# One core of Trainium2, a Fourier layer and an MoE layer: more weight pieces fetched and split in the prologue, one filler more there, and GpSimd's sums for batch 2 held back

## The chip, the cores and the metric

The kernel runs on one core of a Trainium2 chip. The metric is the device time of one execution in microseconds (us), taken as the median of several runs. A core has five engines that work through queues of their own, each in order: TensorE (PE, with its weight loads as PEld), VectorE (DVE), ScalarE (ACT), GpSimd (POOL) and SyncE (SP, which here only issues DMAs). DMAs are also issued from ScalarE's and GpSimd's queues.

## What is computed

For 8 batches of 3008 x 256 numbers, the reference takes a real Fourier transform along the sequence, multiplies by complex weights, adds a bias, shrinks every value towards zero by 0.01, and transforms back. The result, 24064 tokens, goes through a layer of the kind h = x w_in, out = (h cos h) w_out.

```python
X = np.fft.rfft(x, axis=1)
Yr = Xr @ w_r - Xi @ w_i + b_r
Yi = Xr @ w_i + Xi @ w_r + b_i
Yr = np.sign(Yr) * np.maximum(np.abs(Yr) - lam, 0.0)
y = np.fft.irfft(Y, n=x.shape[1], axis=1)
h = x @ w_in
g = h * np.cos(h)
return (g @ w_out).astype(np.float32)
```

The MoE weights w_in (256 x 2048) and w_out (2048 x 256) come as 64-bit floats.

## The kernel before, in words

**Numbers.** Products of 32-bit accuracy are made of three products of a coarser type: each operand is split into a high part (a rounding copy, mostly on ScalarE) and a low part (the operand minus its high part, on VectorE by `rest`, line 328, or on GpSimd by `rest_pool`, line 325).

**The MoE weights** are prepared on the chip, in 16 pieces: 8 of w_in, then 8 of w_out. A piece is loaded raw by GpSimd's queue (`load_f64`, line 255; 512 KB), then `split_f64` turns its 64-bit words into a high and a low 32-bit part, with an Abs on ScalarE (line 268), six instructions on VectorE (lines 269 to 276), a copy on ScalarE (line 277) and a subtraction on VectorE (line 328). Its scratch tile `wa` lies in the buffer "z" for the even ones of the early pieces and in "y" otherwise. Ten pieces (`W_EARLY`) are loaded in the prologue, into the buffers "xp" (`XP_BUFS`, six) which the first batch's input occupied before; piece k + 3 is asked for when piece k is split. Nine are split between the steps of the first batch's transform (`W_AT`) and one more after it. The other six are loaded into the tiles "at", "z" and "Xh" (`load_late_pieces`), and their loads wait for "pc", the transposing products of the first MoE tile; they are split ahead of the steps f = 0, 1, 3, 5, 8 and 11 of that tile (`W_LATE`).

**The order of instructions** comes from three sources. The program emits them in the order of its generators: while one batch's MoE runs, `ahead` lets the next batch's transform come in pieces, with costs that are written by hand. A scheduler then orders each engine's queue by its own estimate of when operands are ready, so an instruction can come well ahead of where it was emitted. Against this, `tc.issue_after(x)` keeps what is emitted under it behind x on x's engine (order only, no wait for x to end). `floor()` (line 317) applies it to the instructions of the MoE step two back: the copy gh on ScalarE, the subtraction gl, and a product; while fewer than two steps exist it holds nothing. Splits are issued under `floor()` and behind `mark["act"]` and `mark["dve"]`, ScalarE's and VectorE's last instructions of the first batch's transform.

**One MoE step** (`moe_step`, `second`) takes 128 of the 2048 hidden columns f for a tile of 512 tokens: six products into ph (lines 923 to 925), on ScalarE u (932), VectorE u (933), ScalarE's sine (935), VectorE's product with h (936), ScalarE's gh (938), gl on VectorE or, for even f, on GpSimd; three steps later six products into po (lines 905, 906, 909). There are 6 tiles of 16 steps per batch.

**The transform.** `stage_a(b)` transforms a batch's input in six blocks c. For batch 1 the blocks are bursts of 16 products each (line 377, tiles pa): three are made in the prologue, as fillers for TensorE (`alone`), three in the first tile (`ahead`, k = 3, 4, 5). Their stores, but for the first, are held until "pc" (`held`, `release`). From batch 2 on GpSimd first makes the sum and the difference of the two halves of a block (`fold`, lines 450 and 451), from tiles xt that its own queue loads (line 442); blocks c + 2 are loaded after the burst of block c. `stage_b(b)` holds the rest: `forward`, `combine` (splitting into Xh and Xl, with sums on GpSimd, lines 594 to 612), `wmix` (lines 660 to 662 and the shrinking, 684 and 686), its own `fold` with GpSimd's lines 699 to 711 and VectorE's transposes (716, 717), and `inverse`/`spread` (739, 740). `stage_c` loads a tile bt, transposes it by products pc (line 377) and splits it into xTh (ScalarE, line 890) and xTl (VectorE, line 891).

Of the kernel before, what the change touches and what calls it, by code (L numbers as in the profile page):

```python
# [13 lines left out]
F32 = mybir.dt.float32  # L14
# [3 lines left out]
U32 = mybir.dt.uint32  # L18
# [10 lines left out]
NFC = FF // 128  # L29
NTT = 6  # L30
SKEW = 3
XP_BUFS = 6
W_AT = (8, 16, 24, 32, 40, 48, 56, 64, 74)
W_ORDER = tuple(range(16))
W_EARLY = 10
W_LATE = (0, 1, 3, 5, 8, 11)
W_AHEAD = 3
POOL_GL = (0, 2)
WARM = 7
# [137 lines left out]
def tile_body(ctx: ExitStack, tc, x, w_r, w_i, b_r, b_i, w_in, w_out,  # L177
              c_fq, c_sig, c_f3, c_ff, c_if, c_iw, c_sgn, out):
    nc = tc.nc
# [80 lines left out]
    def split_f64(k, hi, lo, raw):  # L260

        pair = raw.rearrange("p (n t) -> p n t", t=2)
        v = pair[:, :, 1]
        maq = wk.tile([128, 3, 512], F32, tag="z" if k < W_EARLY and k % 2 == 0 else "y", name="wa", bufs=1)
        m, a, q = (maq[:, j] for j in range(3))
        mu, au, qu = m.bitcast(U32), a.bitcast(U32), q.bitcast(U32)
        ve = nc.vector
        nc.scalar.activation(m, v.bitcast(F32), AF.Abs)
        ve.tensor_scalar(out=m, in0=m, scalar1=F64_TINY, scalar2=F64_HUGE, op0=ALU.max, op1=ALU.min)
        ve.tensor_scalar(out=qu, in0=mu, scalar1=0x07FFFFFF, scalar2=3,  # L270
                         op0=ALU.bitwise_and, op1=ALU.logical_shift_left)
        ve.scalar_tensor_tensor(out=au, in0=v, scalar=0xC0000000, in1=qu,
                                op0=ALU.bitwise_and, op1=ALU.bitwise_or)
        ve.tensor_scalar(out=qu, in0=au, scalar1=0xFF800000, scalar2=None, op0=ALU.bitwise_and)
        ve.scalar_tensor_tensor(out=q, in0=pair[:, :, 0], scalar=2.0 ** -52, in1=q, op0=ALU.mult, op1=ALU.mult)
        ve.tensor_tensor(out=a, in0=a, in1=q, op=ALU.add)
        nc.scalar.copy(hi, a)
        rest(lo, a, hi)
# [15 lines left out]
    raws, mark = [], {}  # L294
# [4 lines left out]
            raws.append(load_f64(raw, words(W_ORDER[len(raws)])))  # L299

    def load_late_pieces():
        for tag, n in (("at", 2048), ("z", 2048), ("Xh", 2304)):
            t = wk.tile([128, n], U32, tag=tag, name="raw", bufs=1)
            for k in range(2):
                raws.append(load_f64(t[:, 1024 * k:1024 * k + 1024], words(W_ORDER[len(raws)]), "pc"))

    def moe_w():
        for k, w in enumerate(W_ORDER):
            load_pieces(k + W_AHEAD)
            with floor(), tc.issue_after(mark["act"].ins), tc.issue_after(mark["dve"].ins):  # L310
                split_f64(k, *halves(w), raws[k])
            yield

# [3 lines left out]
    def floor():  # L317

        ctx = ExitStack()
        for ins in steps[-2] if len(steps) > 1 else ():  # L320
            ctx.enter_context(tc.issue_after(ins.ins))
        return ctx
# [111 lines left out]
    def stage_a(b):  # L434
# [10 lines left out]
                    behind(ins, mark["pc"].ins, "first tile")  # L445

        def fold(c):
            ev[c] = wk.tile([128, 2, 256], F32, tag="xe", name="xe", bufs=2)
            lo, hi = ld[c][:, :, 0], ld[c][:, :, 1]
            nc.gpsimd.tensor_tensor(out=ev[c], in0=lo, in1=hi, op=ALU.add)  # L450
            nc.gpsimd.tensor_tensor(out=lo, in0=lo, in1=hi, op=ALU.subtract)
# [51 lines left out]
        def alone():  # L503
            load(0)
            load(1)
            yield 0.0
            for tag in ("Xh", "Xl"):
                t = wk.tile([128, 2304], F32, tag=tag, name="x1", bufs=1)
                for k in range(2):
                    c = len(ld)  # L510
                    ld[c] = t[:, 1024 * k:1024 * k + 1024].rearrange("p (i g d) -> p i g d", i=2, g=2)
                    nc.sync.dma_start(t[:, 1024 * k:1024 * k + 1024], x[b, :, 1024 * c:1024 * (c + 1)])
            for c in range(3):
                yield from burst_of([c])

        def begin():
# [437 lines left out]
    with ExitStack() as first:  # L954
        pool["pro"] = first.enter_context(tc.tile_pool(name="pro", bufs=1))
        pool["a0"] = early.enter_context(tc.tile_pool(name="a0", bufs=1, side="right"))
        idle = pool["pro"].tile([128, 512], F32R, tag="st", name="idle", bufs=1)
        nc.vector.memset(idle.bitcast(F32), 0.0)
        turn0 = pool["pro"].tile([128, 1], F32, name="turn0", bufs=1)
        nc.scalar.activation(turn0, idle[:, :1].bitcast(F32), AF.Sin)  # L960

        def warm(n):
            p = ps.tile([128, 512], F32, tag="o0", name="pz", bufs=1)
            for _ in range(n):
                mm(p, idle[:, :128], idle, start=True, stop=True)

        warm(WARM)
        fi[0] = pool["pro"].tile([96, 2, 96], F32, name="fi", bufs=1)
        stage_a0()
        load_constants()  # L970
        stages["a"] = stage_a(1)
        side_a = stages["a"].alone()
        next(side_a)
        split = 0
        stages[0] = stage_b(0)
        for i, _ in enumerate(stages[0].first()):
            if i == 0:
                load_pieces(2)
                with tc.issue_after(mark["x0"].ins):
                    load_split_constants()  # L980
            if i == 4:
                with tc.issue_after(mark["a0", 1].ins):
                    sum_fourier_w()
                    bounds()
            if split < len(W_AT) and i >= W_AT[split]:
                next(mw)
                split += 1
        for _ in side_a:
            pass
        next(mw)  # L990
        with tc.issue_after(mark["act"].ins), tc.issue_after(mark["dve"].ins):
            split_fourier_w()
        for _ in range(len(W_AT) + 1, W_EARLY):
            next(mw)
    del pool["pro"]
    pool["mo"] = ctx.enter_context(tc.tile_pool(name="mo", bufs=2, reuse_waits="tile"))
# [10 lines left out]
    def ahead(b):  # L1007

        nxt = b + 1 < NB
        if b == 0:  # L1010
            stages[1] = stage_b(1)
        g = fourier(b + 1) if nxt else iter(())
        for t in range(NTT - 1):
            got = 0.0
            if b == 0 and t == 0:
                yield 3.0
                for k in (3, 4, 5):
                    for c in stages["a"].one(k):
                        got += c
                        yield c  # L1020
                mark["ph"] = None
            yield from stage_c(b, t + 1)
            c = 0.0
            while got < share(b) or isinstance(c, Hold):
                c = next(g, None)
                if c is None:
                    break
                got += c
                yield c
            yield None  # L1030
        yield from g
        if nxt:
            yield GAP
            yield from stage_c(b + 1, 0)
            if b + 2 < NB:
                yield from quiet()
                yield from stages[b + 2].forward(0)
# [57 lines left out]
```

## Time and profile before

| | |
|---|---|
| Median of 3 runs | 2630.61 us (2622.96 to 2635.15) |
| The profiled execution's own time | 2636.05 us |
| Its span, first to last instruction | 2634.3 us |
| Mean granted TensorE clock | 0.992 |
| Busy in the span | PE 2571.2 us (98%), DVE 1943.9 (74%), ACT 1630.0 (62%), POOL 976.7 (37%) |
| DMA | 283.11 MB, mean 107 GB/s |

Busy shares are of the whole span; the stretches in it have different limits. The granted clock is the share of TensorE's full speed, 1.00 or 0.50 at any moment. In the lists, what stands in brackets after an instruction is the idle time of its engine before it and what ended it. A wait for several things is put down to the one that came last.

### The profile page before, as it was taken

The numbers are of one execution on the slowest core, as the hardware profiler recorded it, in microseconds if no ns is written. First come the engines' busy times: TensorE is split into PE (matmuls) and PEld (weight loads), VectorE is DVE, ScalarE is ACT, GpSimd is POOL, SyncE is SP. The second block draws the span as 40 slices with busy tenths as digits, with TensorE's granted clock in tenths as the row PEclk, the third lists the DMA queues.
The fourth block names the chain that finished last, engine by engine and source line by source line (L and its number), as shares of the span: only waits on it lengthen the run. The fifth ranks groups of instructions, "written<-read, shape, count | busy, mean of one in ns | idle before, by whom it ended". The sixth has DMA issues, their size and how long they took to land.

```text
span 2634.3 us, 42943 instructions
## 1 busy us (share of the span) xinstructions
PE 2571.2 (98%) x15961; PEld 2072.1 (79%) x15961; DVE 1943.9 (74%) x3089; ACT 1630.0 (62%) x3003; POOL 976.7 (37%) x946
## 2 busy tenths in 40 slices
PE   9899899999999999999999999999999999999999
PEld 7478678877788777887778877888778888888888
DVE  5688667877768777687776877778776777766665
ACT  5565556665666556656566565665666666666665
POOL 1124443444424443244433445334432333422222
PEclk9999999999999999999999999999999999999999
DMA  6534435354434443334442544326432343210000
GB/s 209 179 102 130 137 109 147 87 146 131 119 86 112 140 128 102 95 108 129 128 117 79 138 133 135 89 87 164 129 100 89 93 111 116 69 38 31 17 25 16
DMA packets 172953, 283.11 MB, mean 107 GB/s; under 512 B 15608, under 2 KB 114200, under 8 KB 169160
## 3 DMA queue, kind: packets, MB, share of 16 engines
q1 hardware_dynamic: 161896, 243.78, 32.9%
q0 software_dynamic: 10112, 35.53, 4.3%
q8 instruction: 126, 2.06, 0.3%
q10 hardware_dynamic: 736, 1.05, 0.1%
q14 instruction: 83, 0.68, 0.1%
HBM read 149.76 MB, written 130.55 MB: 106 GB/s over the span
## 4 chain that ended last, share of the span: by engine, by line
PE 81%; DVE 9%; ACT 3%; DMA 2%; issue 2%; POOL 1%; SPq 0%; DVEq 0%; ACTq 0%; POOLq 0%
PE ph L923 12%; PE po L905 11%; PE ph L924 11%; PE ph L925 11%; PE po L906 11%; PE po L909 11%; PE pw L660 2%; PE pw L661 2%; PE pw L662 2%; DVE u L936 2%; DVE u L933 2%; PE pc L377 1%; PE pb L377 1%; DVE Xl L328 1%; PE pw L656 1%
## 5 line engine op out<-in xcount | busy, mean ns | idle before, releaser
L325 POOL TENSOR_TENSOR gl<-u,gh 128x512 fp32r<-128x512 f32 (+1 forms) x384 | 501.4, 1306 | 1135.4 <-ACT gh L938 942.8
L935 ACT ACTIVATE u<-u 128x512 f32<-128x512 f32 (+1 forms) x768 | 478.1, 623 | 392.7 <-DVE u L933 391.8
L933 DVE SCALAR_TENSOR_TENSOR u<-ph,u 128x512 f32<-128x512 f32 (+1 forms) x768 | 513.6, 671 | 248.3 <-ACT u L932 247.2
L936 DVE TENSOR_TENSOR u<-ph,u 128x512 f32<-128x512 f32 (+1 forms) x768 | 518.0, 675 | 236.6 <-ACT u L935 225.4
L905 PE MATMUL po<-gh,wout 128*128 128x512 f32 (+1 forms) x1536 | 602.4, 392 | 28.0 <-ACT gh L938 28.0
L938 ACT CAST gh<-u 128x512 fp32r<-128x512 f32 (+1 forms) x768 | 467.8, 609 | 257.7 <-DVE u L936 254.6
L923 PE MATMUL ph<-xTh,win 128*128 128x512 f32 (+1 forms) x1536 | 605.2, 394 | 9.3 <-DVE u L936 7.6
L932 ACT ACTIVATE u<-ph 128x512 int32<-128x512 f32 (+1 forms) x768 | 447.7, 586 | 262.4 <-PE ph L925 255.9
L924 PE MATMUL ph<-xTl,win 128*128 128x512 f32 (+1 forms) x1536 | 597.2, 389 | 0.1
L925 PE MATMUL ph<-xTh,win 128*128 128x512 f32 (+1 forms) x1536 | 596.6, 388 | 0.0
L906 PE MATMUL po<-gh,wout 128*128 128x512 f32 (+1 forms) x1536 | 595.5, 388 | 0.0
L909 PE MATMUL po<-gl,wout 128*128 128x512 f32 (+1 forms) x1536 | 476.3, 388 | 0.3 <-POOL gl L325 0.2
L923 PEld LDWEIGHTS ph<-xTh,win 128*128 128x128 f32 x1536 | 290.0, 189 | 101.0 <-DVE u L936 22.5
L905 PEld LDWEIGHTS po<-gh,wout 128*128 128x128 f32 x1536 | 289.4, 188 | 100.6 <-ACT gh L938 38.5
L328 DVE TENSOR_TENSOR gl<-u,gh 128x512 fp32r<-128x512 f32 (+1 forms) x384 | 297.8, 776 | 79.6 <-ACT gh L938 73.5
L925 PEld LDWEIGHTS ph<-xTh,win 128*128 128x128 f32 x1536 | 290.2, 189 | 57.3
L909 PEld LDWEIGHTS po<-gl,wout 128*128 128x128 f32 x1536 | 287.2, 188 | 60.8 <-issue 4.9
L924 PEld LDWEIGHTS ph<-xTl,win 128*128 128x128 f32 x1536 | 290.3, 189 | 51.1 <-DVE xTl L891 0.6
L906 PEld LDWEIGHTS po<-gh,wout 128*128 128x128 f32 x1536 | 289.7, 189 | 50.9
L709 POOL TENSOR_TENSOR odd<-st 128x184 f32<-128x184 f32 (+1 forms) x112 | 67.4, 604 | 147.2 <-DVE st L686 117.0
L328 DVE TENSOR_TENSOR Xl<-z,Xh 128x384 fp32r<-128x384 f32 x112 | 110.3, 1013 | 12.0 <-ACT Xh L594 8.9
L660 PE MATMUL pw<-Xh,wf 128*128 128x384 f32 x336 | 115.5, 344 | 2.4 <-ACT Xh L609 2.2
(123 smaller groups left out, 2453.1 us busy)
## 6 DMA issues: line engine op xcount, KB each, us to landing
scrF<-at SPq DMA_DIRECT2D x28, 1024.0 KB
z<-scrF SPq DMA_DIRECT2D x112, 256.0 KB
scrT<-tr SPq DMA_DIRECT2D x56, 512.0 KB
y<-scrT SPq DMA_DIRECT2D x112, 256.0 KB
bt<-scr SPq DMA_DIRECT2D x94, 256.0 KB
scr<-ao SPq DMA_DIRECT2D x84, 256.0 KB
scr<-bo SPq DMA_DIRECT2D x224, 96.0 KB
out_dram<-ob SPq DMA_DIRECT2D x80, 256.0 KB
```

The source lines that it names most:

```text
L325: return nc.gpsimd.tensor_tensor(out=lo, in0=x, in1=hi.bitcast(F32), op=ALU.subtract)
L905: mm(po[e][:, :n], wo[0][:, 0, f, es], gh[:, :n], start=f == 0, stop=False)
L906: mm(po[e][:, :n], wo[0][:, 1, f, es], gh[:, :n], start=False, stop=False)
L909: mm(po[e][:, :n], wo[0][:, 0, f, es], gl[:, :n], start=False, stop=f == NFC - 1)
L923: mm(h, win[:, 0, c, fs], th[:, c, :n], start=c == 0, stop=False)
L924: mm(h, win[:, 0, c, fs], tl[:, c, :n], start=False, stop=False)
L925: ins = mm(h, win[:, 1, c, fs], th[:, c, :n], start=False, stop=c == 1)
L932: nc.scalar.activation(k[:, :n], h, AF.Identity, bias=0.25, scale=1.0 / TWO_PI)
L933: nc.vector.scalar_tensor_tensor(out=u[:, :n], in0=h, scalar=1.0 / TWO_PI, in1=k[:, :n], op0=ALU.mult, op1=ALU.subtract)
L935: nc.scalar.activation(u[:, :n], u[:, :n], AF.Sin, bias=HALF_PI, scale=TWO_PI)
L936: product = nc.vector.tensor_tensor(out=u[:, :n], in0=h, in1=u[:, :n], op=ALU.mult)
L938: step = [nc.scalar.copy(gh[:, :n], u[:, :n])]
```

## The change

More raw buffers "xp" (nine in place of six); thirteen pieces loaded in the prologue in place of ten. Eleven are split in the prologue's own code, and the next two ahead of f = 0 and f = 1, where nothing of a floor holds them and their raw data are the prologue's. The last three are loaded after "pc" (in "at" and "z") and split ahead of f = 3, 6 and 9. From piece 9 on a split is no longer ordered behind `mark["act"]`. Block 3 of batch 1 is made in the prologue too. For batch 2 alone, GpSimd's sums are emitted under `floor()`. The room for descriptors of GpSimd's DMAs is set to 4096 bytes per partition, where it stood at its default.

```diff
-XP_BUFS = 6
+XP_BUFS = 9
-W_EARLY = 10
-W_LATE = (0, 1, 3, 5, 8, 11)
+W_EARLY = 13
+W_BEFORE = 11
+W_LATE = (0, 1, 3, 6, 9)
...
-        maq = wk.tile([128, 3, 512], F32, tag="z" if k < W_EARLY and k % 2 == 0 else "y", name="wa", bufs=1)
+        maq = wk.tile([128, 3, 512], F32, tag="z" if k < W_BEFORE and k % 2 == 0 else "y", name="wa", bufs=1)
...
     def load_late_pieces():
-        for tag, n in (("at", 2048), ("z", 2048), ("Xh", 2304)):
-            t = wk.tile([128, n], U32, tag=tag, name="raw", bufs=1)
-            for k in range(2):
+        for tag, m in (("at", 1), ("z", 2)):
+            t = wk.tile([128, 2048], U32, tag=tag, name="raw", bufs=1)
+            for k in range(m):
...
-            with floor(), tc.issue_after(mark["act"].ins), tc.issue_after(mark["dve"].ins):
+            with floor(), tc.issue_after(mark["act" if k < len(W_AT) else "dve"].ins), tc.issue_after(mark["dve"].ins):
                 split_f64(k, *halves(w), raws[k])
...
         def fold(c):
+            with floor() if b == 2 else ExitStack():
+                sums(c)
+
+        def sums(c):
             ev[c] = wk.tile([128, 2, 256], F32, tag="xe", name="xe", bufs=2)
...
-            for c in range(3):
+            for c in range(4):
                 yield from burst_of([c])
...
-        next(mw)
         with tc.issue_after(mark["act"].ins), tc.issue_after(mark["dve"].ins):
             split_fourier_w()
-        for _ in range(len(W_AT) + 1, W_EARLY):
+        for _ in range(len(W_AT), W_BEFORE):
             next(mw)
...
-                for k in (3, 4, 5):
+                for k in (4, 5):
...
-    nc = _bacc.Bacc("TRN2", target_bir_lowering=False, num_devices=1)
+    nc = _bacc.Bacc("TRN2", target_bir_lowering=False, num_devices=1,
+                     dynamic_dma_scratch_size=4096)
```

## Rows read from the trace of the kernel before

**Rows 1.** Stretches of the span: each engine's busy us, granted clock, DMA.

```profile
core 0: us, PE busy (x) PEld busy (x) DVE busy (x) ACT busy (x) POOL busy (x), PEclk, DMA share, GB/s
105.60:140.00 34.40, 20.73 (x144) 11.20 (x141) 24.14 (x35) 13.39 (x25) 13.71 (x15) 0.75 0.69 217
140.00:175.00 35.00, 33.01 (x226) 26.30 (x225) 32.03 (x54) 22.55 (x41) 7.33 (x6) 1.00 0.39 106
...
283.00:301.00 18.00, 11.55 (x39) 8.98 (x39) 14.77 (x23) 10.80 (x21) 9.14 (x8) 0.81 0.34 104
301.00:354.00 53.00, 53.00 (x354) 41.49 (x354) 36.60 (x61) 30.81 (x56) 20.66 (x21) 1.00 0.48 139
354.00:366.00 12.00, 6.91 (x22) 5.52 (x21) 11.26 (x16) 5.65 (x11) 7.91 (x7) 0.72 0.24 75
```

**Rows 2.** TensorE's waits from 105 to 142: us in total, times, longest.

```profile
PE ph L923 <- DVE u L936: 6.3, 2, 5.6
PE pc L367 <- DMA bt<-scr: 3.3, 1, 3.3
...
PE ph L923 <- ACT xTh L890: 1.2, 1, 1.2
```

**Rows 3.** Timeline near 118, ScalarE: start us, us, instruction, idle before and releaser.

```profile
118.24 0.67 ACT L268 ACTIVATE wa<-raw 128x512 f32<-128x512 f32 x1 [5.55 <-DMA raw<-in_dram]
```

**Rows 4.** Timeline from 125 to 136, VectorE, GpSimd and TensorE.

```profile
125.83 1.74 DVE L269 TENSOR_SCALAR wa<-wa 128x512 f32<-128x512 f32 x1 [0.73 <-ACT wa L268]
125.99 1.28 POOL L450 TENSOR_TENSOR xe<-xt 128x512 f32<-128x512 f32 x1
...
135.61 0.79 PE L923 MATMUL ph<-xTh,win 128*128 128x512 f32 x1 [5.64 <-DVE u L936]
```

**Rows 5.** Instructions on wa alone: stretch, us, DVE busy, ACT busy, clock, DMA.

```profile
103.00:112.00 9.00, 4.04 (x7) 1.31 (x2) 0.85 0.54 143
...
125.80:133.60 7.80, 7.57 (x6) 0.01 (x1) 0.76 0.82 246
```

**Rows 6.** Stretches at half clock, with the columns of rows 1.

```profile
109.30:116.10 6.80, 5.27 (x72) 3.62 (x71) 2.07 (x4) 1.69 (x3) 3.94 (x6) 0.50 0.42 88
126.40:129.80 3.40, 3.40 (x16) 0.75 (x16) 3.30 (x4) 0.36 (x1) 2.21 (x2) 0.50 1.06 305
133.20:140.00 6.80, 4.39 (x10) 3.47 (x11) 5.88 (x11) 4.30 (x8) 0.00 (x0) 0.50 0.13 32
293.60:300.40 6.80, 5.66 (x14) 4.69 (x15) 4.86 (x8) 4.25 (x9) 3.54 (x4) 0.50 0.38 132
358.50:365.30 6.80, 5.53 (x14) 4.60 (x15) 6.06 (x9) 4.28 (x10) 3.56 (x3) 0.50 0.32 108
```

**Rows 7.** Timeline from 273 to 295, GpSimd, VectorE and TensorE.

```profile
273.15 1.29 POOL L450 TENSOR_TENSOR xe<-xt 128x512 f32<-128x512 f32 x1 [5.56 <-DMA xt<-in_dram]
...
279.98 0.45 DVE L717 STREAM_TRANSPOSE tr<-odd 128x256 f32<-128x256 f32 x1 [6.96 <-POOL odd L709]
...
294.74 0.79 PE L905 MATMUL po<-gh,wout 128*128 128x512 f32 x1 [4.87 <-ACT gh L938]
```

**Rows 8.** TensorE's waits from 450 us to the end.

```profile
PE po L905 <- ACT gh L938: 15.5, 10, 2.1
```

**Rows 9.** VectorE alone, 95.0 to 118.9: stretch, us, DVE busy, clock, DMA.

```profile
95.00:118.90 23.90, 8.35 (x15) 0.86 0.64 187
```

**Rows 10.** The stretch ahead of the first reader of the sums, and that reader.

```profile
250.00:260.00 10.00, 10.00 (x48) 8.56 (x47) 8.48 (x16) 5.43 (x10) 4.46 (x5) 1.00 0.45 154
...
263.78 0.64 PE L377 MATMUL pa<-xe,ff 64*64 64x512 f32 x1
```

**Rows 11.** GpSimd's DMA issues: how many, KB each, median us to landing.

```profile
xt<-in_dram POOLq DMA_DIRECT2D x36, 512.0 KB, 5.6
raw<-in_dram POOLq DMA_DIRECT2D x16, 512.0 KB, 7.6
```

**Rows 12.** TensorE's products pa alone, 116 to 118: us, PE busy, clock, DMA.

```profile
116.00:118.00 2.00, 1.92 (x16) 0.97 1.01 365
```

## The prediction

> **What bounds the kernel now.** I read the page's busy shares first: TensorE is busy 2571.2 of 2634.3 us, so time can only come out of its idle time and out of stretches at the lower of its two clock levels. The table of stretches says where these lie [rows 1]: the head from 105.6 to 140, where the first MoE products start (20.73 of 34.40 us busy, granted clock 0.75), the rest of that tile to 175 (33.01 of 35), and two holes, at 283 to 301 (11.55 of 18, clock 0.81) and 354 to 366 (6.91 of 12, clock 0.72). The list of waits tells what ends the idle time in the head: the loads of the first tile (3.3 us), ScalarE's copy of it (1.2) and above all VectorE's product u (6.3 in two waits) [rows 2]. Two causes stand behind u. ScalarE, which takes its instructions in order, sat 5.55 us on the first late weight piece, whose load is only allowed after the first tile [rows 3]; the first step's own ScalarE work is queued behind it. Then a VectorE instruction that splits the next piece started at 125.83 and took 1.74 us, beside GpSimd's first sum for batch 2 at 125.99; TensorE's next product started at 135.61, after 5.64 us of nothing [rows 4]. Over that stretch six split instructions took 7.57 us; the piece before took 4.04 for seven, so about 3.5 for six [rows 5]. The head paid for its idle time a second time, in three pieces at granted clock 0.50, the lower level of 1.2 GHz, each after such idle time [rows 6].
>
> The hole at 283 to 301 is a chain through three queues [rows 7]. GpSimd stands 5.56 us on the landing of a load for batch 2, because a sum (line 450) is the next thing in its queue; behind it waits stage_b's own fold, work that is ready. VectorE waits 6.96 us for these at line 717, with the u of the MoE steps behind that, and 5 us (4.87) of TensorE are gone when gh comes late. The hole at 354 to 366 has the same pattern, one quarter of the batch later. In the batches after that the same kind of wait at line 905 costs 15.5 us in ten waits, none over 2.1 [rows 8].
>
> **The change, part by part.**
>
> *Head: raw pieces and splits.* To be had there: 34.40 - 20.73 = 13.7 us idle, half of the 5.27 + 3.40 + 4.39 us that TensorE worked at half clock, 6.5, and 2.0 idle to 175: 22.2 together [rows 1, 6]. Three splits of 4.04 us VectorE and 1.31 us ScalarE each [rows 5] move ahead of the first products; 12.1 us of VectorE. What hides them: VectorE is busy 8.35 of the 23.90 us from 95.0 to 118.9 [rows 9], 15.5 us free, mostly because it waits for the last inverse transforms and for the first tile. Piece 9 may now start before the last of these, since its order after ScalarE's copies is dropped. If this cover were gone, the 12.1 us would stand before the first products. The three loads (median 7.6 us from issue to landing [rows 11]) move to before the first tile, where ScalarE no longer waits for one: the 5.55 us go. I cost their issues on GpSimd's queue at nothing, since that queue then only waits for the first tile's load. Three raw buffers more also let loads 0 to 2 start without waiting for the input's readers; that may delay loads beside them, 0 to 5 us by the wait for a landing in rows 3; I take 0, for TensorE's waits name none of the constants that these loads run beside [rows 2].
>
> *The fourth filler.* The burst is 1.92 us of TensorE [rows 12]; it moves from 116 into the 3.3 us wait for the first tile [rows 2]. Its two copies and its store go with it; the store is held like its neighbours' and adds nothing to SP's queue ahead of the first tile. VectorE has no part in it.
>
> What stays in the head, with bounds: of the tile's wait 3.3 - 1.9 = 1.4; the copy 1.2; the 2.0 to 175; time at half clock, 0 to 6.5, I take 1.0, as the idle time left is in short pieces; ScalarE's share of three splits among the last copies before the first tile, 0 to 3 x 1.31 = 3.9, taken as one, 1.3; a split ahead of the tile's low half (xTl) in VectorE's queue, 0 to 4.0, taken as 1.0. That is 7.9, so the head gives **14.3**.
>
> *GpSimd's sums held back.* The floor puts each pair of sums behind the gl of a step two or three back, so ahead of the burst that reads it but no longer in front of a load's landing. The first pair leaves the head for the ten microseconds or so before its readers at 263.78 [rows 10]; the other two leave 273 and 337 for the like place a quarter of the batch later. What could be late next is that burst, whose sums are now made only shortly before it. To be had: (18 - 11.55) + (12 - 6.91) = 11.5 idle and half of 5.66 + 5.53, 5.6, at half clock: 17.1 [rows 1, 6]. What stays: two waits as in later batches, 15.5 / 10 each, 3.1 [rows 8]. What is new: three pairs beside VectorE at other places. A pair cost VectorE 7.57 - 3.5 = 4.1 in the head; at the first new place it is idle 10 - 8.48 = 1.5 of 10 us [rows 10], so up to 2.6 each, 7.8 for three, and at least 0. I take 1.0 each, 3.0, because TensorE has steps in store there that it lacked in the head. **11.0**.
>
> The Trainium skill (SBUF — State Buffer, Who interferes with whom) speaks against this part: GpSimd has only the port pair that it shares with VectorE, and an instruction of VectorE with two SBUF inputs, or in a two-port mode, blocks against GpSimd's reads, whoever came first. By that rule the sums' price is only carried elsewhere. The trace agrees in the head, with 1.74 us for the split's instruction beside a sum of 1.28 [rows 4].
>
> *Wait for "act" dropped, late pieces in two tiles in place of three, later splits at f = 3, 6, 9:* costed at nothing; they are covered by the 2.0 us left above.
>
> *The descriptor store of GpSimd's DMAs cut to 4096:* the trace shows no wait for room in it. Below nothing is excluded, a store gives nothing back; above, an issue could wait for a landing, 5.6 to 7.6 us [rows 11]. I take 0, since in the trace issues follow each other without any such wait.
>
> **Sum.** 14.3 + 11.0 = 25.3 us. The profiled execution took 2636.05 us (span 2634.3), so 2610.8 for one like it; it stands 5.4 over the median of the three runs, 2630.61 (2622.96 to 2635.15), from which the same sum gives **2605**.
>
> **The rivals.**
>
> *1. The sums collide wherever they run (17%).* Each of the three pairs costs TensorE what it cost at 125.8: 5.64 us [rows 4] and half of 4.39 at half clock [rows 6], 7.8; three make 23.5. Then 14.3 + 17.1 - 3.1 - 23.5 = 4.8, and the time is 2626: no change. For it: VectorE is 85% busy at the new place. Against it: the pair at 337 ran between 301 and 354, where TensorE was busy for all 53 us [rows 1]. By the Trainium skill's rule above this is what the change would come to.
>
> *2. The change doesn't do what it says in the head (16%).* The order of instructions is the scheduler's; pieces 11 and 12 may fall behind the first products, or split work may come ahead of the tile. Then the head gives only the filler's 1.9 and the sums' 4.1, 6.0, and with 11.0 the time is 2614. For it: only VectorE's and ScalarE's last marks order them. Against it: 15.5 us free.
>
> *3. Slower (7%): the smaller descriptor store makes GpSimd wait at its issues.* Price: one wait of 5.6 us in that queue cost 17.1 / 2 = 8.6 us of TensorE [rows 7]. Lost gain and half a per cent, 25.3 + 13.2 = 38.5, are reached from the fifth such wait; there are 36 loads of xt alone [rows 11]. With six it is 2605 + 52 = 2657. Against it: loads come in pairs, far apart, and nothing waits today. The Trainium skill (SBUF — State Buffer, SBUF size: 192, 224, or 256?) gives the store as 16 KiB; no row shows its size.
>
> **How the numbers follow.** 60% for the forecast. Its own range goes by the bounds: everything taken as cost gone but 1.4 and 1.2 gives 36.7 us (2594); late copies and splits in full and 7.8 for collisions give 25.3 - 5.6 - 4.8 = 14.9, and some of the half-clock time besides, 2618. To hold 8 in 10 it is widened to rival 1 above, 2628, and by a little below, 2592; that leaves out rival 3 and the rest of the tails. A measurement of this kernel tells about 0.5%, 13 us, from no change. Faster by over that (below 2617): nearly all of the forecast, two thirds of rival 2, little of rival 1: 0.68. Slower: rival 3, 0.07. The same: 0.25.
>
> **What would show it.** Right: ScalarE's split of piece 10 no longer waits for a raw load; from 105 to 140 TensorE is busy over 28 us; no sum for batch 2 before about 250 us; no 5 us idle at line 905 before 366, and VectorE's wait at line 717 under 2 us. Rival 1: line 717 or u late at the new places, with stretched VectorE instructions beside the sums. Rival 2: splits of pieces 11 and 12 after the first ph. Rival 3: GpSimd's issues longer than now, or idle with "issue" before them. A first product later than 112.75 by over 3 us would make the head's step wrong.

## The result and the profile after

The kernel with the change takes **2604.6 us** (median of 4 runs, 2600.94 to 2608.73), against 2627.51 for the kernel before beside it (4 runs, 2622.96 to 2635.15): a ratio of 0.9906, 95% interval [0.9889, 0.9923]. That is faster by 22.9 us, where 25.3 were forecast and 2605 predicted. The profiled execution took 2601.79 us, with a mean granted clock of 0.997 (0.992 before).

The page of the kernel after: its span, and busy us, share of the span and instructions of each engine.

```profile
span 2600.0 us, 42935 instructions
...
PE 2559.2 (98%) x15961; PEld 2065.8 (79%) x15961; DVE 1937.6 (75%) x3089; ACT 1628.9 (63%) x3003; POOL 979.7 (38%) x946
```

The same five stretches as in [rows 1], with the same columns.

```profile
105.60:140.00 34.40, 28.97 (x264) 16.05 (x264) 22.68 (x38) 21.46 (x41) 7.04 (x9) 0.90 0.76 232
140.00:175.00 35.00, 33.80 (x170) 26.54 (x170) 30.20 (x50) 22.80 (x41) 8.53 (x7) 1.00 0.45 113
283.00:301.00 18.00, 17.62 (x162) 13.92 (x161) 13.41 (x21) 11.01 (x20) 6.36 (x6) 1.00 0.45 115
301.00:354.00 53.00, 50.40 (x261) 39.72 (x260) 42.92 (x66) 30.65 (x57) 26.05 (x24) 1.00 0.50 142
354.00:366.00 12.00, 12.00 (x115) 10.10 (x114) 9.57 (x16) 6.92 (x14) 10.25 (x10) 1.00 0.12 45
```

In the head TensorE is busy 28.97 us where it was 20.73, and the two holes of [rows 1] are gone from their places. But there is still half-clock time in the head, and it follows new waits. Two stretches of the kernel after, columns as before:

```profile
101.40:104.80 3.40, 3.40 (x11) 2.04 (x10) 2.76 (x5) 2.03 (x5) 0.00 (x0) 0.50 0.20 58
118.50:125.30 6.80, 5.86 (x22) 2.58 (x22) 2.50 (x4) 2.07 (x4) 0.96 (x2) 0.50 1.00 345
```

TensorE's waits from 95 to 142 in the kernel after (us in total, times, longest), to be read against [rows 2]:

```profile
PE ph L928 <- ACT xTh L895: 3.5, 1, 3.5
PE pi L785 <- DVE yf L772: 2.6, 1, 2.6
PE pc L368 <- DMA bt<-scr: 1.1, 1, 1.1
PE pc L378 <- DMA bt<-scr: 0.4, 1, 0.4
```

The waits for u (6.3 us) are gone and the first tile's load fell from 3.3 to 1.1 and 0.4. In their place stand ScalarE's high half of the tile, 3.5 us instead of 1.2, and 2.6 us for VectorE's yf, where before has 0.5. Before also has 2.5 us in which a filler's products wait for ScalarE's copies, and that is gone too (TensorE's waits from 95 to 142, kernel before):

```profile
PE pa L367 <- ACT ao L486: 2.5, 1, 2.5
...
PE pi L780 <- DVE yf L767: 0.5, 1, 0.5
```

The timeline of after shows where the two new waits come from (start, us, instruction, idle before it and its releaser).

```profile
99.79 0.68 DVE L772 TENSOR_TENSOR yf<-pt,sig 96x512 f32<-96x512 f32 x1
100.52 0.67 PE L785 MATMUL pi<-yf,fi 96*96 96x512 f32 x1 [2.61 <-DVE yf L772]
...
116.78 0.62 ACT L278 CAST wout<-wa 128x512 fp32r<-128x512 f32 x1 [2.63 <-DVE wa L277]
117.30 1.07 ACT L491 COPY ao<-pa 128x512 f32<-128x512 f32 x2
118.26 1.09 ACT L895 CAST xTh<-pc 128x512 fp32r<-128x512 f32 x2
119.39 0.79 PE L928 MATMUL ph<-xTh,win 128*128 128x512 f32 x1 [3.51 <-ACT xTh L895]
```

ScalarE stands 2.63 us on the last step of a split (the cast of a piece of w_out), then makes two copies of the filler, and only then the tile's high half. The first MoE product starts at 119.39, where it started at 112.75 before.

GpSimd's sums for batch 2: the line's instructions within the first 500 us of the kernel after (count; shortest, median and longest ns; first and last start).

```profile
L455 POOL TENSOR_TENSOR xe<-xt x8: 1288/1302/1766, 241.6 to 381.0; 128x512 f32<-128x512 f32 x8
```

The first now runs at 241.6. Two smaller holes are left: the one at 273 to 295 [rows 7] has become this (timeline, TensorE):

```profile
280.45 0.50 PE L910 MATMUL po<-gh,wout 128*128 128x512 f32 x1 [3.10 <-ACT gh L943]
```

The other, 2.55 us, ends at 341. At both the granted clock stays at 1.00. From 450 us on, TensorE's waits of [rows 8] are fewer too, which the forecast did not have:

```profile
PE po L910 <- ACT gh L943: 6.0, 8, 1.2
```

**Where the gain lies.** Every MoE step ends in VectorE with the product u (line 936 of before), 96 of them a batch, 768 in all, and the steps come in the same order in all these kernels. So the end of the same step can be set against each other. As the kernel before I take a second execution of the old order for this, from the experiment "store_only" below. In us, against that execution (minus is earlier; steps and products counted from 0):

| | start of TensorE's product 470 (at 94 to 95 us) | step 32 (at 231 to 242 us) | step 95, the last of batch 0 (447 to 472) | step 767, the last |
|---|---|---|---|---|
| before, profiled | +0.1 | +0.8 | +1.8 | +7.1 |
| after | +1.2 | -9.4 | -15.5 | -25.7 |
| sums_only | -0.2 | -3.6 | -11.3 | -13.4 |
| no_sums | +1.0 | -7.6 | -10.6 | -17.4 |
| all_sums | +0.1 | -10.5 | -22.9 | -34.3 |

TensorE's first 480 products are the same and in the same order in all kernels of this document, and from product 120 to product 470 the offset changes by 0.03 us at most. So the first column is scatter of an execution's first 20 us, and what the head itself gives is step 32 less this column: 10.6 us in the change, 3.4 in sums_only, 8.6 in no_sums, 10.6 in all_sums. The change and all_sums have the same edits in the head and agree there; cast_last and cast_sums below, also alike in it, are 1.2 apart.

The two rows of the old order tell how far two executions of the same instructions part: 1.8 us in batch 0, and 5.3 more behind it. So a reading of the head, taken like this, is good to about 1 us, one in batch 0 to about 2; one of the later batches is not.

### The profile page after: what moved, and what is told of

Its sections match the earlier page's. It is cut to its first block, busy times and chain, and to the rows that moved or that the text cites. A ratio compares the mean times of both kernels' runs of the same rounds, so it can differ in the third digit from the quotient of the medians.

```text
span 2600.0 us, 42935 instructions
## 1 busy us (share of the span) xinstructions
PE 2559.2 (98%) x15961; PEld 2065.8 (79%) x15961; DVE 1937.6 (75%) x3089; ACT 1628.9 (63%) x3003; POOL 979.7 (38%) x946
## 4 chain that ended last, share of the span: by engine, by line
PE 83%; DVE 9%; ACT 3%; DMA 2%; issue 2%; POOL 1%; SPq 0%; ACTq 0%; DVEq 0%; POOLq 0%
PE ph L928 12%; PE po L910 12%; PE ph L929 11%; PE ph L930 11%; PE po L914 11%; PE po L911 11%; PE pw L665 2%; PE pw L667 2%; PE pw L666 2%; DVE u L941 2%; DVE u L938 2%; PE pb L378 1%; PE pc L378 1%; DVE Xl L329 1%; PE pw L661 1%
## 5 line engine op out<-in xcount | busy, mean ns | idle before, releaser
L910 PE MATMUL po<-gh,wout 128*128 128x512 f32 (+1 forms) x1536 | 599.7, 391 | 13.4 <-ACT gh L943 13.4
L714 POOL TENSOR_TENSOR odd<-st 128x184 f32<-128x184 f32 (+1 forms) x112 | 68.9, 617 | 121.5 <-DVE st L691 118.9
```

The costliest lines, as they stand in the source:

```text
L910: mm(po[e][:, :n], wo[0][:, 0, f, es], gh[:, :n], start=f == 0, stop=False)
```

## The experiments

Theory: the head gives its part because splits stand before the tile, the sums theirs because they are no longer in front of a load, the smaller descriptor store nothing. Rivals: the three of the prediction; and, once the head was seen to give less than forecast, the question which instruction ahead of the tile costs it.

**The sums alone, on the kernel before** (sums_only).

```diff
         def fold(c):
+            with floor() if b == 2 else ExitStack():
+                sums(c)
+
+        def sums(c):
```

> The kernel before with GpSimd's sums for batch 2 held back and nothing else. My theory (the sums block GpSimd's queue on a load's landing, VectorE's behind it, and stretch VectorE's split work in the head): about 11 us less by the two holes and up to 4 less in the head, so 2613 to 2617 against 2627.5 before. Rival (they collide with VectorE wherever they run): 2624 or more, and new TensorE waits near the sums' new places.

Measured: 2615.86 us, 0.9952 [0.9938, 0.9967], that is 11.2 us less. By the table 3.4 of it lie in the head, where the first pair no longer stands beside the splits [rows 4], and 7.7 in the rest of batch 0, for which the sum had 11.0. TensorE's wait for gh, from 175 to 430 (us in total, times, longest):

```profile
PE po L909 <- ACT gh L942: 7.3, 4, 3.3
```

VectorE's wait for GpSimd's fold, from 250 to 430:

```profile
DVE tr L721 <- POOL odd L713: 4.0, 3, 2.6
```

That wait, 6.96 us in [rows 7], is now 2.6 at most, and TensorE's, 4.87 there, is 3.3. The mechanism is the one forecast.

**The change without it** (no_sums): the kernel after, with `fold` the plain `sums`.

```diff
-            with floor() if b == 2 else ExitStack():
-                sums(c)
+            sums(c)
```

> The changed kernel without the hold on the sums. My theory: the sums go back into the head and in front of their loads, the two holes near 290 and 355 are there again, 2614 to 2620 against 2604.6. Rival (the head is what counts, the holes were filled by other means): 2607 or less.

Measured: 2610.34 us, 0.9937 [0.9922, 0.9952], less than the 2614 to 2620 that were expected. TensorE's wait for gh from 175 to 430 is back in it:

```profile
PE po L909 <- ACT gh L942: 10.8, 3, 5.5
```

And VectorE's from 250 to 430:

```profile
DVE tr L721 <- POOL odd L713: 14.0, 5, 6.8
```

So within the change the floor is worth 2610.34 - 2604.6 = 5.7 us, half of its 11.2 alone. Part of it is won only once: in the head the floor alone wins 3.4 us, the rest of the change alone 8.6, and both together 10.6, not 12.0. Another part is lost again at batch 3's sums (all_sums below).

**The smaller descriptor store alone** (store_only).

```diff
-    nc = _bacc.Bacc("TRN2", target_bir_lowering=False, num_devices=1)
+    nc = _bacc.Bacc("TRN2", target_bir_lowering=False, num_devices=1,
+                     dynamic_dma_scratch_size=4096)
```

> The kernel before with the descriptor store at 4096 and nothing else, so the same order of instructions. My theory: no difference, within 5 us of before, and GpSimd's issues last as long as before; its profile also shows how far a second execution of the old order lies from the first. Rival a (waits for room): 2640 or more. Rival b (the 15 us that the changed kernel's trace gains after the first batch come from the store): 2612 to 2616.

Measured: 2625.15 us, 0.9990 [0.9980, 1.0001] with 10 runs: no difference. TensorE's waits are much like those of before [rows 2, 8]; from 95 to 175, where before has 7.6 us in three waits for u:

```profile
PE ph L923 <- DVE u L936: 8.6, 2, 7.3
```

And after 450:

```profile
PE po L905 <- ACT gh L938: 14.3, 10, 1.9
```

Rival 3 falls, and so does rival b above, that the store brings the gain behind batch 0.

**The floor for every batch's sums** (all_sums). Holes after 366 us in the kernel after (1.46, 1.08 and 2.01 us at 385, 395 and 403) lie beside batch 3's sums, which nothing holds.

```diff
-            with floor() if b == 2 else ExitStack():
+            with floor():
```

> The changed kernel with the sums of batches 3 to 7 held back as well. My theory: GpSimd's waits on loads in front of sums (43 us over 18 waits after 450 us in the trace of before) go, and the later waits at po get shorter: 2597 to 2605 against 2604.6. Rival (those waits never reach TensorE, the sums then collide with VectorE later): 2605 to 2612.

Measured: 2595.57 us, 0.9881 [0.9864, 0.9897], 9.0 below the change and 1.4 below the range that was expected. The stretch from 390 to 412, columns as in [rows 1]:

```profile
390.00:412.00 22.00, 21.80 (x126) 17.57 (x125) 16.16 (x26) 15.67 (x29) 5.06 (x4) 1.00 0.49 131
```

The three holes are gone; 22.9 us are won by step 95, where the change had 15.5. So the mechanism found at batch 2 holds for batch 3 too. Behind that the floor adds little: of the later batches' sums, GpSimd in the kernel after stands 42.1 us in 16 waits on loads after 450 us (its list of waits):

```profile
POOL xe L455 <- DMA xt<-in_dram: 42.1, 16, 3.8
```

In all_sums that line is not in the list. Yet from step 95 to the last it wins 11.4 us on the old order, and the change 10.2. So most of those 42.1 us are idle time of an engine that nobody waits for there; what the rest costs can't be told from the scatter.

**The filler back in the first tile** (filler_back).

```diff
-            for c in range(4):
+            for c in range(3):
                 yield from burst_of([c])
...
-                for k in (4, 5):
+                for k in (3, 4, 5):
```

> The changed kernel with its fourth filler back in the first tile (blocks 0 to 2 of batch 1 in the prologue, 3 to 5 after). My theory (the burst fills the wait for the first tile, 1.5 us after against 3.3 before): TensorE's wait at pc is about 3.3 again, the copies of ScalarE ahead of xTh are fewer by 1.1 us, a net of 0.5 to 2.5 worse: 2605 to 2607 against 2604.6. Rival (its copies cost at xTh what it gives at pc): 2604 or less, with the wait at xTh under 2.5 us in place of 3.5.

Measured: 2606.01 us, 0.9914 [0.9896, 0.9932]. It is in the expected range, but against the change's 2604.6 the difference is within the error. Its head shows the trade (TensorE's waits, 95 to 175):

```profile
PE pc L368 <- DMA bt<-scr: 2.7, 1, 2.7
PE ph L928 <- ACT xTh L895: 1.9, 1, 1.9
```

The tile's load costs 2.7 instead of 1.1 us, and the high half 1.9 instead of 3.5, since two copies less stand ahead of it on ScalarE. The burst shortens the one wait and lengthens the other by as much, so no idle time goes by it. What it wins comes behind the first product, when the burst is no longer among the first tile's steps: its head gives 7.8 us (-7.5 at step 32, +0.3 at product 470), 2.8 less than the change's, where the burst itself takes 1.9 [rows 12].

**The wait for "act" kept for all late splits** (act_kept), with thirteen pieces loaded as in the change.

```diff
-            with floor(), tc.issue_after(mark["act" if k < len(W_AT) else "dve"].ins), tc.issue_after(mark["dve"].ins):
+            with floor(), tc.issue_after(mark["act"].ins), tc.issue_after(mark["dve"].ins):
```

> The changed kernel with every split ordered behind ScalarE's last copy of the transform, as before. My theory (splits 9 and 10 ahead of VectorE's yf are what made the last inverse transforms 5 us later): the first product comes 2 to 4 us earlier than 119.4, and the time falls by 1 to 3 us: 2601.5 to 2603.5. Rival (the split work then queues up right before the first tile, whose copy must wait for it): the first product at 119 or later, 2604.6 to 2609.

Measured: 2610.94 us, 0.9928 [0.9906, 0.9949], a wide run (2604.68 to 2613.86), 6.3 over the change, with intervals that overlap. The first product starts at 119.25, not 2 to 4 us earlier as expected: the rival was right. The cover that the prediction counted on, the time before the last inverse transforms, can't be used then, and the splits crowd ahead of the tile (TensorE's waits, 95 to 175):

```profile
PE ph L928 <- ACT xTh L895: 9.6, 1, 9.6
PE ph L929 <- DVE xTl L896: 3.0, 1, 3.0
```

The order that was dropped, costed at nothing as an edit of its own, is thus worth 5.6 us of the head: 5.0 (-5.9 at step 32, -0.9 at product 470) against 10.6.

**Eleven pieces before, five behind** (eleven): nothing of the twelfth and thirteenth piece before the first products.

```diff
-W_EARLY = 13
+W_EARLY = 11
...
-W_LATE = (0, 1, 3, 6, 9)
+W_LATE = (2, 3, 5, 7, 9)
...
-        for tag, m in (("at", 1), ("z", 2)):
-            t = wk.tile([128, 2048], U32, tag=tag, name="raw", bufs=1)
+        for tag, m in (("at", 2), ("z", 2), ("Xh", 1)):
+            t = wk.tile([128, 2304 if tag == "Xh" else 2048], U32, tag=tag, name="raw", bufs=1)
```

> The changed kernel with eleven raw pieces early in place of thirteen; five late ones (two each in at and z, one in Xh), split ahead of f = 2, 3, 5, 7, 9. Question: what splitting pieces 11 and 12 ahead of the first products is worth. My theory (they delay the first product by about 3.5 us, but every split in the first tile's steps costs TensorE more): first product at 115 to 117, VectorE over 90% busy from 120 to 160 and TensorE's waits at u and po back, 2605 to 2610. Rival (only the wait of ScalarE for the raw load mattered, and a later place cures it as well): 2601 to 2604.

Measured: 2617.04 us, 0.9953 [0.9938, 0.9968], 12.4 over the change and 7.0 over the range that was expected. VectorE has no room left in the stretch from 140 to 175 (columns as in [rows 1]):

```profile
140.00:175.00 35.00, 32.08 (x161) 24.70 (x160) 34.76 (x55) 21.24 (x39) 6.05 (x7) 1.00 0.47 112
```

It is busy 34.76 of 35 us, against 30.20 in the change. Its head gives 3.5 us (-3.0 at step 32, +0.5 at product 470) where the change's gives 10.6. So what the two pieces cost ahead of the tile is less than what they cost behind it. By step 95 it has lost 4.5 us more on the change, which this run doesn't explain; its fifth late piece also lies in another tile (Xh).

**The splits behind the last inverse transforms** (yf_first): the pieces from the tenth on wait for two yf of VectorE's last group, against the 2.6 us.

```diff
-            with floor(), tc.issue_after(mark["act" if k < len(W_AT) else "dve"].ins), tc.issue_after(mark["dve"].ins):
+            late = mark["yf", 3, 0 if k == len(W_AT) else 2] if k >= len(W_AT) else mark["act"]
+            with floor(), tc.issue_after(late.ins), tc.issue_after(mark["dve"].ins):
...
-                    nc.vector.tensor_tensor(out=y ...
+                    mark["yf", q, j] = nc.vector.tensor_tensor(out=y ...
```

> The changed kernel with piece 9 behind VectorE's first yf of the last inverse transform and the pieces after it behind its second one. My theory (the splits ahead of yf made the last inverse transforms late; the tile then waits for split 12 by ScalarE's order): the 2.6 us wait at pi goes, the wait at xTh grows by most of it, 2603 to 2606 against 2604.6. Rival (the transforms set the first product): first product 3 us earlier, 2600 to 2602.

Measured: 2605.93 us, 0.9918 [0.9902, 0.9935]: no difference from the change that can be told. In its profile the wait for yf is down to 0.5 us and the first product starts at 112.64; the wait for the high half did not grow, as had been expected, but fell from 3.5 to 2.9, and one for the tile's low half comes in (TensorE's waits, 95 to 142):

```profile
PE ph L930 <- DVE xTl L897: 2.9, 1, 2.9
PE ph L929 <- ACT xTh L896: 2.9, 1, 2.9
```

It stands at -12.9 at step 32, but at -1.2 already at product 470, where the change is at +1.2: its head gives 11.7, some 1 us more than the change's, which is about what two executions part. At the last step it stands at -23.4, where the change has -25.7; its waits for gh after 450 are longer:

```profile
PE po L911 <- ACT gh L944: 11.6, 10, 1.9
```

So the order around yf is what makes the wait for yf, and it puts off the first product; that the head of the change loses time by it up to step 32 is not shown, nor that removing it gains time over the whole kernel.

**The last cast behind the tile** (cast_last): the thirteenth split's cast and its subtraction wait for the tile's two halves.

```diff
-        nc.scalar.copy(hi, a)
-        rest(lo, a, hi)
+        with ExitStack() as tile:
+            for name in ("high", "low") if k == W_EARLY - 1 else ():
+                tile.enter_context(tc.issue_after(mark[name].ins))
+            nc.scalar.copy(hi, a)
+            rest(lo, a, hi)
...
+            if first:
+                mark["high"], mark["low"] = high, low
```

> The changed kernel with the last two instructions of split 12 (ScalarE's cast, VectorE's rest) behind the first tile's xTh and xTl. My theory (xTh stands in ScalarE's queue behind the cast of split 12, which waits 2.6 us for VectorE): first product 1.5 to 2.5 us earlier than 119.4, wait at xTh under 2 us, 2602 to 2604. Rival (xTh must wait for the raw pieces anyway): within 0.5 us of the changed kernel at the first product, 2604.6.

Measured: 2601.2 us, 0.9898 [0.9884, 0.9913], 3.4 below the change, with intervals that overlap. The first product starts at 115.62, 3.8 us earlier than in the change (1.1 of that stand at product 470 already), and the wait for the high half is back at what it was in [rows 2] (TensorE's waits, 95 to 142):

```profile
PE pc L371 <- DMA bt<-scr: 2.6, 2, 1.6
...
PE ph L934 <- ACT xTh L898: 1.2, 1, 1.2
PE pc L381 <- DMA bt<-scr: 0.7, 1, 0.7
```

So the 2.3 us that this wait grew by are the cast's doing: ScalarE waits in its queue for VectorE's split, with the tile's copy behind. Part of it is lost again on the tile's load, 2.6 and 0.7 us where the change has 1.1 and 0.4; the head gives 11.5 us (-11.4 at step 32, +0.1 at product 470) against 10.6, a gain within the scatter, and at the last step this execution stands at -25.1, the change at -25.7. So the cause of the longer wait is shown, a gain in time by its removal is not. Holding both pieces wholly behind the tile was not tried: the tile's buffers take the place of raw pieces that the splits must first have read.

**All three together** (three: yf_first, cast_last and all_sums) and **two of them** (cast_sums: cast_last and all_sums).

> Both orders together, and the sums of all batches held back. My theory: the parts add, 2595.6 less 2 to 5 us: 2590 to 2594. Rival (VectorE has no room before the first tile, so each order only moves the wait): 2595 to 2598.

> The order of cast_last with the sums of all batches held back, without the order of yf_first. My theory: the gains of the two runs add, 2595.6 less 1 to 3.4: 2592 to 2595. Rival (the order of yf_first gives its 3 us of the head here as well): 2595 to 2598, over 1 us behind the run with all three.

Measured: three 2593.5 us, 0.9869 [0.9854, 0.9884]; cast_sums 2594.93, 0.9870 [0.9854, 0.9886]. Both beat the kernel before and the change. Beside all_sums' 2595.57 they win 2.1 and 0.6 us, which the intervals do not tell apart: the floor for all sums carries nearly the whole of it. Both times lie where the theories had them, but in the head the orders don't add: three gives 11.6 us there, cast_sums 10.3, yf_first 11.7, cast_last 11.5, and all_sums, with neither order, 10.6. That is the rival's case, that each order only moves the wait.

## Why the prediction was right, and where it was not

The total is right, 2604.6 for 2605. The terms are not: head 14.3 and sums 11.0 were forecast, and by the table 10.6 and 15.5 - 9.4 = 6.1 came by step 95, 16.7 together. What is left of the 22.9 us, about 6, comes from the batches behind, which had no term (a rough figure: medians against single executions). Two terms that were some 4 and 5 us too large and one left out have met in the right number, and that is luck.

**Head, the cover and the order of splits: right in kind.** Three splits fit ahead of the first products, ScalarE no longer stands 5.55 us on a raw piece [rows 3], and the waits for u are gone. Gone too are the 2.5 us of a filler's products, which the prediction counted among its 13.7 us and didn't name; they are gone in filler_back as well, so by the splits' move and not the filler's. "eleven" shows that the move of the last two pieces is what matters most, 7.1 of the 10.6 us, "act_kept" that the dropped order makes the cover of [rows 9] usable. Rival 2 had the splits fall behind the first products; they did not. Its other half, split work ahead of the tile, did happen, but the head gave 10.6 us and not the 6.0 of that rival.

**Head, what stays: mis-sized.** 7.9 us were to stay. The profile of after has 34.40 - 28.97 = 5.4 and 1.2 us idle in the two stretches, 2.6 at yf before them, and half of 3.40 + 5.86, 4.6, at half clock: 13.8, which is 5.9 more. (By this count 22.2 - 13.8 = 8.4 us were won, by the steps' ends 10.6; the two counts differ by 2.) Three steps of the prediction failed:
- "Time at half clock, 0 to 6.5, I take 1.0, as the idle time left is in short pieces": it is 4.6. The idle time left is 2.61 us at 98 and 3.51 at 116, and a piece at granted clock 0.50 (1.2 GHz) follows each. The largest error, 3.6.
- The cover itself, "mostly because it waits for the last inverse transforms": VectorE's free time was there, but the splits of two pieces stood around a yf that TensorE needed, 2.6 us of a wait that no term had. In yf_first it falls to 0.5.
- "ScalarE's share of three splits among the last copies before the first tile, 0 to 3.9, taken as one, 1.3": with the copy's 1.2 that made 2.5, and the wait is 3.5. Here the duration of the work was counted, 1.31, and not that ScalarE stands in its queue 2.63 us for VectorE before a 0.62 us cast. cast_last shows it.

The tile's wait (1.4 forecast, 1.1 + 0.4) is right; the split ahead of the low half (1.0) cost nothing, as no wait for xTl is in the list. By the prediction's own test, a first product over 3 us later than 112.75, the head's step is wrong: it is 6.6 later, or 5.5 if both are counted from product 470. Yet step 32 ends 9.4 earlier, because the steps that follow no longer stop for u.

The term for raw loads 0 to 2, taken as 0, was right, though the row it was read from could not show it: [rows 2] begin at 105 us, these loads at 16. Over the ten profiles with nine raw buffers, product 470 starts 0.1 us later than in store_only on average (-1.2 to +1.2).

**The filler: the gain there, by another way.** It was to win 1.9 us in the tile's wait. It takes 1.6 from that wait, but its two copies lie ahead of the tile's high half on ScalarE and lengthen that one by 1.6; "its two copies go with it" was said and not priced. The gain, 2.8 us of the head against filler_back, 1.4 by the medians and within their error, comes behind the first product.

**The sums: the mechanism right, the size not.** Taking the sums out of the place in front of a landing shortens the chain of [rows 7], as sums_only and no_sums show from both sides. Where the size went can be read by counting TensorE's 15961 products in order of their start, against store_only: the change stands at -9.4 us from the 1320th to the 1520th, at -15.4 at the 1640th, behind the first hole, and at -19.1 at the 1980th, behind the second. So 9.7 of the 17.1 us are won at the two holes. By the 2340th it is back at -15.5: 3.6 are lost at the smaller holes beside batch 3's sums, for which the prediction had no term. all_sums, which removes them, goes from -19.7 to -21.3 over the same products; no_sums wins 1.4 at the two holes (-7.6 to -9.0).

Two waits of 1.55 us were to stay, 3.1; those left are 3.10 and 2.55 us. At the first of them GpSimd doesn't stand on a load. Its sums of `combine`, which the floor doesn't touch, run beside VectorE's instructions ahead of u, and of these line 691 takes 1.38 us where it took 0.55 at 247.97 (timeline of the kernel after):

```profile
274.63 2.57 POOL L606 TENSOR_TENSOR z<-z 128x384 f32<-128x384 f32 x2 [0.76 <-DVE Xl L329]
274.94 1.38 DVE L691 TENSOR_TENSOR st<-st,cl 128x384 f32<-128x384 f32 x1
```

No half-clock time follows the two waits in this execution. In sums_only it follows both waits of that kind, 3.31 and 3.06 us long (columns as in [rows 1]), so that it is the change that keeps the clock up there is not shown:

```profile
286.40:289.70 3.30, 3.30 (x8) 2.78 (x9) 3.02 (x4) 2.43 (x6) 2.20 (x2) 0.50 0.42 164
347.80:351.10 3.30, 2.80 (x7) 2.42 (x8) 3.30 (x7) 2.73 (x6) 1.50 (x2) 0.50 0.40 159
```

VectorE's wait for the fold was to fall under 2 us, and in the kernel after, from 250 to 430, it is 3.8 at the longest (list of waits):

```profile
DVE tr L722 <- POOL odd L714: 6.3, 3, 3.8
```

The first sum runs at 241.6 us, not after 250. And a collision, taken as 1.0 us, cost VectorE 2.5 at the first new place (timeline of the kernel after, VectorE and GpSimd; then that VectorE line over the whole run, shortest, median and longest ns):

```profile
244.45 3.00 DVE L689 TENSOR_SCALAR cl<-st,blo,bhi 128x384 f32<-128x384 f32 x1
...
244.69 2.54 POOL L456 TENSOR_TENSOR xt<-xt 128x512 f32<-128x512 f32 x2
```

```profile
L689 DVE TENSOR_SCALAR cl<-st,blo,bhi x122: 431/479/3003, 33.4 to 2240.7; 128x384 f32<-128x384 f32 x122
```

From step 32 to step 36 VectorE's products u lose 2.5 us against the old order in the change (-9.4 to -6.9) and in sums_only (-3.6 to -1.1), and nothing in no_sums (-7.6 both). That is the upper bound that the prediction gave, 2.6. But TensorE pays none of it: its 1320th and its 1520th product, on either side of the place, both start 9.4 us earlier, it has no gap over 0.5 us there, and the clock does not fall. Rival 1 is right that the collision moves along, and wrong on its price, 7.8 us for each pair.

The Trainium skill (SBUF — State Buffer, Who interferes with whom) states that of an instruction of VectorE in a two-port mode and one of GpSimd, the one that issues first blocks the other fully, not partly. The trace agrees on the full blocking: 3.00 us against the line's median of 0.479, longer by about the 2.54 us of GpSimd's two subtractions. It doesn't show in which mode VectorE's instruction ran, and by the recorded starts VectorE's, the one held up, came first (244.45 against 244.69).

**The descriptor store: right**, nothing.

**The later batches: not forecast.** The change gains 10.2 us more from the end of batch 0 to the last step against store_only, and its waits after 450 are 6.0 us in total, against 14.3. GpSimd's order is the same there in both. Two executions of one order part by 5.3 us in the same part, so half of the 10.2 may be chance; and store_only's profiled execution lies 2.3 us over its median, the change's 2.8 under its own. The orders of the other engines are not the same: from 480 us on, 69 of TensorE's some 13100 products, 18 of VectorE's instructions and 32 of ScalarE's stand in other places than in store_only, though no edit touches these batches. no_sums has the order of the change there and wins 6.8 us; sums_only has the old one and wins 2.1. So the scheduler's other order is a candidate, which no run tested; yf_first, with 43 products moved, wins only 2.3. What the rest is stays open; the sums of the later batches it is not, as all_sums wins hardly more there.

## What to carry to other kernels

An instruction that waits for a landing should not stand in a queue in front of work that is ready; once that is found for one batch, look for it in every batch. When work is moved ahead of a milestone, count for each in-order engine not only how long the moved instructions run but how long they stand waiting for another engine, with the milestone's own instruction behind them. A total that comes out right proves no term of its sum: set the ends of the same product side by side in both traces, counted from a product that no edit has reached yet, and see where each part came. And read a delay from the engine that bounds the kernel: 2.5 us that VectorE lost cost TensorE nothing.

## What was not expected of the hardware

A VectorE instruction of 0.479 us took 3.00 beside two of GpSimd's that followed each other, the length of both and not of one. The idle time that TensorE had before its clock fell doesn't tell alone whether it falls: after 3.51 us at 116 a stretch at 0.50 followed, after 3.10 us at 277 none, as the stretch around that hole shows (kernel after, columns as in [rows 1]):

```profile
266.00:290.00 24.00, 20.85 (x95) 17.03 (x94) 21.52 (x32) 14.17 (x28) 11.29 (x10) 1.00 0.38 99
```

In all_sums two waits for the same instruction, gh, were 2.71 and 2.70 us long, and the clock fell behind the second alone (the stretches right behind them, same columns):

```profile
279.00:282.40 3.40, 3.35 (x15) 2.57 (x16) 3.40 (x6) 2.15 (x5) 2.18 (x2) 1.00 0.41 159
339.30:342.70 3.40, 3.40 (x9) 2.82 (x10) 3.40 (x5) 2.18 (x5) 2.16 (x2) 0.51 0.41 161
```

And two executions of the same order of instructions, 1.8 us apart after 472 us, were 7.1 apart at the end.
